# Attention beside a long convolution on one core: narrower convolution matmuls, kv stores in load order, and an earlier table for the short filter

## The chip, the cores and the metric

The kernel runs on one core of one Trainium2 chip. The metric is the device time of one execution in microseconds (us); the time before is the median of three runs, 858.24 us. TensorE is called PE (PEld is its weight load), VectorE DVE, ScalarE ACT, GpSimd POOL, and SyncE, which issues most DMAs, SP. "PEq", "SPq" and so on are the sequencers of these engines.

## The reference

Two independent halves, each over S = 2048 rows and D = 640 channels in bfloat16, are concatenated along the channels:

```python
# A: a short filter, a gate, and a long causal convolution per channel
k_shift = sum_t k[s - t, :] * shift_k[:, t]            # t = 0..3
kv = k_shift * v
y[s, c] = sum_{u <= s} kv[u, c] * ssm_k[c, s - u]      # by FFT in the reference
y = y + kv * ssm_D
a = q * y
# B: softmax attention, 32 heads of 20 channels
q, k, v = (x @ wqkv), split into heads
o = softmax(q k^T * 20**-0.5) v
b = o @ wo
out = concatenate([a, b], axis=-1)
```

## The kernel before

**A planner writes the program.** The class `Prog` keeps a list of instructions for each engine and a modelled clock for each. `build_kernel` walks PE's modelled time forward and, step by step, picks what PE does next; DVE, POOL and SP get their work when the model says that it is ready. The result is a fixed order on each engine, with semaphore waits between them. Constants such as `CQ`, `ZTH`, `ZLO`, `KV0` and `KVS` are the planner's costs, thresholds and due times, so that a changed constant reorders instructions throughout.

**Attention.** Queries are taken in four chunks of 512 (qc), heads in eight groups of four (g), keys in 16 blocks of 128 (kb). A score tile is one head, 128 keys by 512 queries: there are 2048 of them, counted from 0 in the order in which PE makes them. Two or three tiles fill PSUM banks 0 to 2 or 3 to 5 (`S_task`, L619). ACT turns two or three at once into exps in SBUF (`EXP_task`, L661). One tile in seven is given to DVE instead: L681 takes it out of PSUM, and a chain of L716, L717, L718, L719, L721 and L711 or L713, mostly for two tiles at once, makes its exp. `PV_task` (L739) multiplies the exps with V into bank 6; DVE moves that out (L749), and later steps normalise, transpose and multiply with Wo. 36 slots of 512 columns hold exps until PV has read them (32 until the convolution starts).

**Projections.** Q, K (L473) and V (L522) are made from the transposed x as needed, g by g. Their due times are in units of four tiles. DVE copies them from PSUM (L462, L527).

**The first half.** `k_load` brings chunks of 512 rows of k (transposed by the DMA) and of v. `C_task` (L550) applies the short filter on PE: for each of four shifts it multiplies with a diagonal matrix, the table `Dg`, which POOL builds by one instruction from the identity and the filter `SK` (L592). DVE multiplies by v into the tile `kvst` (L570), and SP writes it to `kvr_scratch` in HBM, its rows turned within blocks of 32. There are 20 C tasks, due at `KV0 + KVS * n`. POOL issues the DMAs that copy the long filter into `kext_scratch` (L579 to L590).

**The convolution.** Once all is stored, `conv_setup` clears the tile `KVr` on POOL (L926), loads 80 channels of kv (`kvr_load`), and then 40 tasks of 16 channels run between the other work (`conv_task`, L974): 128 matmuls each, with 128 columns of weights from shifted rows of the long filter (`hk_load`, four DMAs for four channels). POOL arranges the moving columns (`kvx_build`, L948). Each matmul but the first of a task reads twice as many columns as it has data: the second half comes from a tile of zeros, `KVZ`, and adds nothing, but keeps PE's array streaming:

```python
rhs = sub(KVX[i], [[(2 - i) * KVX_E - p, 1 if st else 2], [64, 2], [2, n]], p)
o = sub(bank[MISC], [[-16 if u + x else 16, 1 if st else 2], [256, 2], [1, n]], (4 * u + x) * 16 + d)
```

Here n is 16 - d, with d from 0 to 3. Besides these, `zeros` (L381) multiplies a zero tile with 512 zero columns where PE waits and its planned share of streaming within 3.4 us (`share`) is low. DVE takes the result out (L990, L991, L993); after every tenth task `A_start` loads q, POOL multiplies (L1015) and SP stores the first half.

**What sets the order around the change.** At the start, SP issues the loads of x (`x_load`, transposed), then weights, then SK, k and v. POOL's queue is in the order of `setup_pool`: memsets, the kext DMAs, HD, then Dg. Each DMA on a semaphore waits for the one before it on the same semaphore.

Of the kernel before, what the change touches and what calls it, by code (L numbers as in the profile page):

```python
# [25 lines left out]
NAQ = 6  # L26
# [4 lines left out]
OBS = 20  # L31
NXB = 3
KBV, KBW, LONE = 13, 12, 16
CQ = 0.026
KV0, KVS, VQ, CONVE, ZTH, AGE, WAIT3 = 52, 2.5, 5, 80, 2.1, 40, 0.2
ZST = 6
# [4 lines left out]
PKX, PAT = 0.56, 0.42  # L41
DMAX = 2.0
ZSL, ZLO = 0.45, 1.8
# [43 lines left out]
class Prog:  # L87
# [140 lines left out]
    def dmas(self, eng, pairs, dsem, reads=(), writes=(), slow=1, turn=False):  # L228
# [18 lines left out]
        c = 0.475 * len(pairs)  # L247
# [29 lines left out]
def build_kernel(nc, A_q, A_k, A_v, A_shift_k, A_ssm_k, A_ssm_D, B_x, B_wqkv, B_wo, out):  # L277
# [3 lines left out]
    with ExitStack() as es:  # L281
# [30 lines left out]
        HK_E, KVR_E, KVX_E, Y_E, AST_E = 4 * HKW, 64 * 80, 16 * 64, 16 * 160, 160  # L312
# [14 lines left out]

        WKV = carve(NCC * 2 * D).rearrange("p (c n) -> p c n", c=NCC)
# [3 lines left out]
        kvst = [carve(4 * D).rearrange("p (t d) -> p t d", t=4) for _ in range(2)]  # L332
        pos[0] = 0
        HK = [carve(HK_E) for _ in range(NHK)]
        KVr2 = carve(KVR_E)
# [14 lines left out]
        kvr_d = nc.dram_tensor("kvr_scratch", (S, D), BF16).ap()  # L350
# [49 lines left out]
        for t in range(4):  # L400
            x_load(t, 1)
        x_load(4, 4)
        w_load("sp", [(WKV, D, 2, 0, 160), (WKV, 0, 1, 80, 80), (WQ, 0, 0, 80, 80)], b_Wa, "wa")
# [81 lines left out]
        def prologue():  # L485

            def two(bw, bd):

                bd.w = [t for b in bw for t in b.w]
                bd.r = []  # L490
            for _ in range(ZST):
                zeros(0, 1, True)
            KQ_mm("K", 0, MISC, 0, 384)
            hq, hk = [Buf(), Buf()], [Buf(), Buf()]
            for i, (bk, eng) in enumerate(((4, "dve"), (3, "act"))):
                KQ_mm("Q", 0, bk, 256 * i, 256)
                if i == 0:
                    copy("act", KT[:, 0, 0:384], bank[MISC][:, 0:384], bkb[MISC], hk[0], 0.6)
                copy(eng, QT[:, 0, 256 * i:256 * (i + 1)], bank[bk][:, 0:256], bkb[bk], hq[i], 0.45)
            KQ_mm("K", 0, 5, 384, 128)  # L500
            copy("dve", KT[:, 0, 384:512], bank[5][:, 0:128], bkb[5], hk[1], 0.35)
            two(hq, b_QT[0])
            two(hk, b_KT[(0, 0)])
# [27 lines left out]
        d_kT, d_v, d_kvst = ([DS(n + "0"), DS(n + "1")] for n in ("kT", "v", "kvst"))  # L531
        d_Bs = DS("bs")
        d_kvr, d_sk, d_kext, d_small = DS("kvr"), DS("sk"), DS("kext"), DS("small")
# [6 lines left out]
        def C_task(c, h, bk):  # L540
# [18 lines left out]
            def after():  # L559
                if h < 4:  # L560
                    return
                for t in range(4):
                    bd = Buf()
                    P.dma("sp", ap(kvr_d, [[32 * D, 4], [-D, 32], [1, D]], (c * 512 + t * 128 + 31) * D), kvst[i][:, t, :],
                          d_kvst[i], reads=[b_kvst[i]], writes=[bd])
                    b_kvd.append(bd)
                if c < 2:
                    k_load(c + 2)
# [3 lines left out]
        def setup_pool():  # L572
# [3 lines left out]
            P.dma("sp", SK, ap(A_shift_k, [[KS, 128], [128 * KS, NCC], [1, KS]]), d_sk, writes=[b_SK])  # L576
            k_load(0)
            k_load(1)
# [13 lines left out]
            P.op("pool", lambda e: e.tensor_tensor(  # L592
                Dg, ap(ident, [list(ident.ap[0]), [0, KS], [0, NCC], [1, 128]]),
                ap(SK, [list(SK.ap[0]), [1, KS], [KS, NCC], [0, 128]]), ALU.mult), reads=[b_ident, b_SK], writes=[b_Dg], c=6.0)
# [320 lines left out]
        def conv_setup():  # L915
            allx = [b_WK0, b_WQ0, b_Wa, b_Wb, b_Dg] + b_kT + b_vst + b_kvst
            cv["dead"] = [t for b in allx for t in b.w + b.r]
            cv["HK"] = [Buf(*allx) for _ in range(NHK)]
            cv["KVr"] = Buf(*allx)
# [6 lines left out]
            P.op("pool", lambda e: e.memset(KVr[:, 0:48, :], 0.0), writes=[cv["KVr"]], c=48 * 80 * 0.00095)  # L926
# [6 lines left out]
        def kvr_load(b):  # L933
            P.dmas("sp", [(KVr[32 * a:32 * a + 32, 16 * a:64, :],
                           ap(kvr_d, [[D, 32], [32 * D, 64 - 16 * a], [1, 80]], 80 * b)) for a in range(4)],
                   d_kvr, reads=b_kvd, writes=[cv["KVr"]], slow=2)
# [6 lines left out]
        def kvx_build(t):  # L943
            i = t % 2
            for h in range(2):
                dst = sub(KVX[i].bitcast(U32), [[64, 4], [16, 4], [1, 16]], 256 * h)
                src = sub(KVr2, [[1, 4], [40, 4], [160, 16]], t % 5 * 8 + 4 * h)
                pool_work(lambda e, dst=dst, src=src: e.tensor_copy(dst, src), [cv["KVr"]], [cv["KVX"][i][h]], PKX,  # L948
                          lambda h=h: kvr_load(t // 5 + 1) if h and t % 5 == 4 and t < 39 else None)
# [5 lines left out]
        def conv_task(bt):  # L955
# [3 lines left out]
            for u in range(4):  # L959
# [3 lines left out]
                for x in range(4):  # L963
                    for k in range(8):
# [6 lines left out]
                        rhs = sub(KVX[i], [[(2 - i) * KVX_E - p, 1 if st else 2], [64, 2], [2, n]], p)  # L971
                        o = sub(bank[MISC], [[-16 if u + x else 16, 1 if st else 2], [256, 2], [1, n]], (4 * u + x) * 16 + d)
                        yield (CQ, rd if x + k == 0 else [])
                        P.op("pe", lambda e, o=o, lhsT=lhsT, rhs=rhs, st=st, k=k: e.matmul(  # L974
                            o, lhsT, rhs, start=st, stop=k == 7, skip_group_check=True),
                            reads=rd, writes=[bkb[MISC]], tok=last, c=CQ, st=4 * n / 2400)
# [22 lines left out]
        def A_load(B, tp):  # L999
            i = tp % NAQ  # L1000
            P.dma("sp", Aq[i], ap(q2, [[D, 128], [1, 160]], tp * 128 * D + 160 * B), d_aq[i], writes=[cv["Aq"][i]])

        def A_start(B):

            def go(tp):
                i = tp % NAQ
                q = cv["Aq"][i]
                A_load(B, tp)

                def after():  # L1010
                    P.dma("sp", ap(out2, [[2 * D, 128], [1, 160]], tp * 128 * 2 * D + 160 * B), Aq[i], d_ao[i], reads=[q])
                    if tp + NAQ - 2 < 16:
                        go(tp + NAQ - 2)

                pool_work(lambda e, a=Aq[i], y=Y[B % 2][:, tp, :]: e.tensor_tensor(a, a, y, ALU.mult), [q, cv["Y"][B % 2]], [q], PAT,  # L1015
                          after)

            for tp in range(NAQ - 2):
                go(tp)
# [99 lines left out]
        def dve_run(until):  # L1119
            while True:  # L1120
# [8 lines left out]
                if True:  # L1129
                    fn, rd, wr, c, two = w.steps[w.i]  # L1130
                    t = last_dve[0]
                    last_dve[0] = P.op("dve", fn, reads=rd, writes=wr, c=c, two=two, me=w.steps[w.i])
                    if t and not two:
                        end = st
                        for x in w.steps[w.i:]:
                            if x[4]:
                                break
                            end += x[3] - 0.04
                        if end - st > 0.35:
                            pool_beside(t, st, end)  # L1140
                    w.i += 1
                    if w.i == len(w.steps):
                        works.remove(w)
                        if w.after:
                            w.after()
# [275 lines left out]
```

## Time and profile before

| | |
|---|---|
| median of 3 runs (lowest, highest) | 858.24 us (856.96, 860.21) |
| the profiled execution's own time | 856.55 us |
| its span, first to last instruction | 853.9 us |
| ACT, PE, DVE, POOL busy | 811.3, 819.9, 775.2, 96.4 us |
| exps on ACT (L661): instructions, busy, idle before | 742, 807.8, 26.8 us |
| convolution matmuls (L974) | 5120 |
| zero matmuls (L381) | 230 |
| first exp starts, last exp ends | 10.70, 844.5 us |

A row of a group reads: line, engine, operation, tile written <- tile read, shapes, count, then busy time and mean ns of one, then the engine's idle time just before these instructions and what ended most of it. In the timeline, the first two numbers are start and length, and the bracket holds the idle time before the row's first instruction and its releaser. A busy PE is not a full PE, since matmuls overlap.

### The profile page before, as it was taken

How to read it: one execution, taken by the hardware profiler on the slowest of the kernel's cores; microseconds unless marked ns; L12 is line 12 of the kernel's file. 1: busy time of each engine (PE TensorE's matmuls, PEld its weight loads, DVE VectorE, ACT ScalarE, POOL GpSimd, SP SyncE). 2: the span in 40 equal slices, each digit the busy share in tenths (PEclk: the TensorE clock that was granted, in tenths of full speed). 3: DMA queues.
4: the chain of work that ended last, by engine and by line, in shares of the span. 5: the costliest groups of instructions: out<-in, count | busy, mean ns of one | idle time of the engine just before them, and what ended most of it. 6: DMA issues, size and time to landing. Idle time of an engine off the chain costs nothing.

```text
span 853.9 us, 27281 instructions
## 1 busy us (share of the span) xinstructions
PE 819.9 (96%) x11683; PEld 380.6 (45%) x11694; DVE 775.2 (91%) x1560; ACT 811.3 (95%) x748; POOL 96.4 (11%) x160
## 2 busy tenths in 40 slices
PE   8979999999999999999999999999999999999997
PEld 3433433442255454444535544554544554455422
DVE  1388999999989999998999999999999999999992
ACT  5878799999999999999999999999999999999996
POOL 2020000000111000012211010230110121100011
PEclk9989999999999999999999999999999999999999
DMA  8920110211749967988988796689798888988411
GB/s 171 295 68 2 38 59 16 79 33 32 145 107 201 185 170 169 182 169 183 200 160 173 169 202 146 171 197 199 178 188 157 192 200 192 163 184 182 76 31 46
DMA packets 189463, 121.91 MB, mean 143 GB/s; under 512 B 98048, under 2 KB 188672, under 8 KB 189344
## 3 DMA queue, kind: packets, MB, share of 16 engines
q1 hardware_dynamic: 187152, 117.06, 64.5%
q0 software_dynamic: 736, 2.75, 0.9%
q8 instruction: 92, 1.51, 0.8%
q10 hardware_dynamic: 1456, 0.37, 0.2%
q14 instruction: 27, 0.22, 0.1%
HBM read 106.83 MB, written 10.61 MB: 138 GB/s over the span
## 4 chain that ended last, share of the span: by engine, by line
PE 50%; ACT 33%; DVE 15%; issue 1%; DMA 0%; SPq 0%; DVEq 0%
ACT R L661 33%; PE PS L974 17%; PE PS L619 15%; PE PS L739 8%; PE PS L473 5%; DVE XV L681 3%; DVE XF L721 2%; PE PS L381 2%; PE PS L825 2%; PE PS L522 1%; DVE R L711 1%; DVE ZS L991 1%; DVE ZS L990 1%; DVE R L993 1%; DVE XF L718 1%
## 5 line engine op out<-in xcount | busy, mean ns | idle before, releaser
L661 ACT ACTIVATE R<-PS 128x1024 bf16<-128x1024 f32 (+1 forms) x742 | 807.8, 1230 | 26.8 <-PE PS L619 25.2
L619 PE MATMUL PS<-QT,KT 20*128 20x512 bf16 x2048 | 288.0, 385 | 15.2 <-ACT R L661 7.1
L974 PE MATMUL PS<-R 128*128 128x60 bf16 (+4 forms) x5120 | 212.1, 195 | 0.2 <-DVE R L993 0.2
L681 DVE TENSOR_SCALAR XV<-PS 128x512 uint16<-128x512 f32 x289 | 197.5, 685 | 16.3 <-PE PS L619 13.3
L974 PEld LDWEIGHTS PS<-R 128*128 128x128 bf16 x5120 | 176.0, 98 | 79.0 <-issue 77.7
L739 PE MATMUL PS<-R,V_sb 128*21 128x512 bf16 x2048 | 168.2, 385 | 9.3 <-DVE R L713 5.6
L619 PEld LDWEIGHTS PS<-QT,KT 20*128 20x128 bf16 x2048 | 71.9, 91 | 189.3 <-ACT R L661 131.7
L721 DVE TENSOR_TENSOR XF<-XF 128x1024 bf16<-128x1024 bf16 x145 | 103.6, 716 | 0.3
L718 DVE TENSOR_TENSOR XF<-XF 128x1024 bf16<-128x1024 bf16 x145 | 98.4, 683 | 0.2
L948 POOL COPY R<-R 128x256 uint32<-128x256 uint32 x80 | 51.1, 638 | 377.6 <-DVE XF L721 114.1
L739 PEld LDWEIGHTS PS<-R,V_sb 128*21 128x21 bf16 x2048 | 37.8, 89 | 82.1 <-issue 40.6
L381 PE MATMUL PS<-Zt 128*128 128x512 bf16 x230 | 69.0, 396 | 1.6 <-DVE Zt L375 1.0
L711 DVE TENSOR_TENSOR R<-XF,XV 128x1024 uint16<-128x1024 bf16 x92 | 63.0, 686 | 0.2
L719 DVE TENSOR_SCALAR XF<-XF 128x1024 bf16<-128x1024 uint16 x145 | 60.5, 419 | 0.4
L717 DVE TENSOR_SCALAR XF<-XF 128x1024 bf16<-128x1024 uint16 x145 | 59.9, 420 | 0.1
L716 DVE TENSOR_SCALAR XF<-XV 128x1024 uint16<-128x1024 uint16 x145 | 59.7, 419 | 0.2
L473 PE MATMUL PS<-xT,WQ 128*20 128x512 bf16 (+1 forms) x660 | 51.1, 386 | 1.5 <-DVE XV L681 0.8
L1015 POOL TENSOR_TENSOR R<-R 128x160 bf16<-128x160 bf16 x64 | 31.2, 487 | 160.7 <-DVE XF L719 50.8
L473 PE MATMUL PS<-xT,R 128*20 128x512 bf16 (+2 forms) x660 | 47.3, 378 | 1.1 <-DMA xT<-in_B_x_dram 0.5
L713 DVE TENSOR_TENSOR R<-XF,XV 128x512 uint16<-128x512 bf16 x105 | 40.5, 419 | 0.1
L462 DVE CAST KT<-PS 128x512 bf16<-128x512 f32 (+1 forms) x32 | 21.6, 675 | 14.0 <-PE PS L473 13.6
L749 DVE CAST OT_sb<-PS 128x512 bf16<-128x512 f32 x32 | 21.8, 682 | 12.8 <-PE PS L739 12.8
(54 smaller groups left out, 359.9 us busy)
## 6 DMA issues: line engine op xcount, KB each, us to landing
R<-kext_scratch SPq DMA_DIRECT2D x640, 136.0 KB, 3.7
R<-in_A_v_dram SPq DMA_DIRECT2D x4, 640.0 KB, 6.4
kext_scratch<-in_A_ssm_k_dram POOLq DMA_DIRECT2D x1, 2560.0 KB, 13.2
kvr_scratch<-R SPq DMA_DIRECT2D x16, 160.0 KB
R<-kvr_scratch SPq DMA_DIRECT2D x8, 320.0 KB, 6.2
R<-in_A_q_dram SPq DMA_DIRECT2D x64, 40.0 KB, 3.6
out_dram<-R SPq DMA_DIRECT2D x64, 40.0 KB, 3.2
R<-kvr_scratch SPq DMA_DIRECT2D x8, 240.0 KB, 6.9
```

What stands on the lines that cost most here:

```text
L381: P.op("pe", lambda e: e.matmul(bank[bk], Zt, zrhs, start=start, stop=start, skip_group_check=True), reads=[b_Zt], writes=[bkb[bk]], tok=s ...
L473: ins = e.matmul(bank[bk][32 * i:32 * i + DH, 0:n], Wt[:, cc, off + i * DH:off + (i + 1) * DH], xT[:, cc, x0:x0 + n], start=(cc == 0), sto ...
L619: ins = e.matmul(bank[b0 + i], KT[32 * u:32 * u + DH, g, kb * 128:(kb + 1) * 128], QT[32 * u:32 * u + DH, qs(qc, g), :], start=True, stop= ...
L661: P.op("act", lambda e: e.activation(P_sb[:, s0:s0 + m, :], PS[:, b0 * 512:(b0 + m) * 512].rearrange("p (u q) -> p u q", u=m), ACT.Exp, sc ...
L681: work(0.2, [(lambda e: e.tensor_scalar(V, bank[bk], scale * 1.4426950408889634 * 128.0, 127.0 * 128.0, op0=ALU.mult, op1=ALU.add), [bkb[b ...
L711: last = [(lambda e: e.tensor_tensor(o, Q2, V2, ALU.add), bv + [bq], [b_P[z] for z in zs], two, True)]
L717: (lambda e: e.tensor_scalar(Q, F.bitcast(U16), -128.0, None, op0=ALU.add), [bf], [bq], one, True),
L718: (lambda e: e.tensor_tensor(Q, Q, F.bitcast(U16), ALU.mult), [bf, bq], [bq], two, True),
L719: (lambda e: e.tensor_scalar(F, F.bitcast(U16), a / 16384.0, b / 128.0, op0=ALU.mult, op1=ALU.add), [bf], [bf], one, True),
L721: (lambda e: e.tensor_tensor(Q, Q, F, ALU.mult), [bf, bq], [bq], two, True)] + last, end)
L739: ins = e.matmul(bank[OBANK][32 * u:32 * u + DH + 1, :], V_sb[:, kb, 4 * g + u, :], P_sb[:, slot[4 * b + u], :], start=first, stop=last, t ...
L974: P.op("pe", lambda e, o=o, lhsT=lhsT, rhs=rhs, st=st, k=k: e.matmul(o, lhsT, rhs, start=st, stop=k == 7, skip_group_check=True), reads=rd ...
```

## The change

- **Zero columns.** A convolution matmul reads the second, zero half only for d = 1 and 2, and only where the planned share is under `ZDU`. The planner counts `CQ` for a narrow and `CQD` for a wide one. Thresholds of the zero matmuls move (`ZTH`, `ZSL`, `ZLO`).
- **Prologue.** x's first 512 rows come by two loads of 256, K and Q of the first group in two halves each, with 7 and 4 zero matmuls ahead of them.
- **SK and Dg.** SK's load is issued after x's first eight tiles of 128 rows. Dg's multiply stands ahead of the kext DMAs on POOL. `k_load(1)` moves behind the small loads.
- **kv stage.** `kvst` lies under `KVr` rather than beside the other old tiles, with a semaphore for each row tile (eight in all). C tasks are due at 48 + 2 n rather than 52 + 2.5 n.
- **kv in HBM.** `kvr_scratch` has the order of its loads: for each of eight channel groups, 32 rows of 64 x 80 values. Each of the 16 row tiles is stored by eight DMAs of 80 channels; a load reads one run for each partition.
- **The clearing of KVr** goes in four pieces to the queue of POOL work that the planner puts beside DVE. The q loads and stores of the first half take two row tiles each.
- **Other planner constants**, in the diff's first part.

```diff
-NAQ = 6
+NAQ = 3
-OBS = 20
+OBS = 28
-KBV, KBW, LONE = 13, 12, 16
-CQ = 0.026
-KV0, KVS, VQ, CONVE, ZTH, AGE, WAIT3 = 52, 2.5, 5, 80, 2.1, 40, 0.2
-ZST = 6
+KBV, KBW, LONE = 12, 12, 24
+CQ, CQD, ZDU = 0.0258, 0.0304, 2.1
+KV0, KVS, VQ, CONVE, ZTH, AGE, WAIT3 = 48, 2.0, 5.5, 100, 2.2, 40, 0.2
+ZST = 7, 4
-PKX, PAT = 0.56, 0.42
-DMAX = 2.0
-ZSL, ZLO = 0.45, 1.8
+PKX, PAT = 0.64, 0.49
+DMAX = 2.5
+ZSL, ZLO = 0.3, 1.4
...
-        c = 0.475 * len(pairs)
+        c = (0.475 if len(pairs) < 8 else 0.545) * len(pairs) if not turn else 0.4 + 0.0068 * pairs[0][1].shape[0]
...
+        kvst = [carve(4 * D).rearrange("p (t d) -> p t d", t=4) for _ in range(2)]
         WKV = carve(NCC * 2 * D).rearrange("p (c n) -> p c n", c=NCC)
...
-        kvst = [carve(4 * D).rearrange("p (t d) -> p t d", t=4) for _ in range(2)]
         pos[0] = 0
+        KVr2 = carve(KVR_E)
         HK = [carve(HK_E) for _ in range(NHK)]
-        KVr2 = carve(KVR_E)
...
-        kvr_d = nc.dram_tensor("kvr_scratch", (S, D), BF16).ap()
+        kvr_d = nc.dram_tensor("kvr_scratch", (8, 32, 64, 80), BF16).ap()
...
-        for t in range(4):
-            x_load(t, 1)
+        x_load(0, 2)
+        x_load(2, 2)
         x_load(4, 4)
+        d_sk = DS("sk")
+        P.dma("sp", SK, ap(A_shift_k, [[KS, 128], [128 * KS, NCC], [1, KS]]), d_sk, writes=[b_SK])
...
-            for _ in range(ZST):
-                zeros(0, 1, True)
-            KQ_mm("K", 0, MISC, 0, 384)
...
+            for i, (bq, bk) in enumerate(((4, MISC), (3, 5))):
+                for _ in range(ZST[i]):
+                    zeros(i, 1, True)
+                KQ_mm("Q", 0, bq, 256 * i, 256)
+                copy("dve", QT[:, 0, 256 * i:256 * (i + 1)], bank[bq][:, 0:256], bkb[bq], hq[i], 0.45)
+                KQ_mm("K", 0, bk, 256 * i, 256)
+                copy("act", KT[:, 0, 256 * i:256 * (i + 1)], bank[bk][:, 0:256], bkb[bk], hk[i], 0.45)
...
+        d_kvst = [DS("kvst%d" % n) for n in range(8)]
...
-                    P.dma("sp", ap(kvr_d, [[32 * D, 4], [-D, 32], [1, D]], (c * 512 + t * 128 + 31) * D), kvst[i][:, t, :],
-                          d_kvst[i], reads=[b_kvst[i]], writes=[bd])
+                    P.dmas("sp", [(ap(kvr_d, [[80, 4], [-5120, 32], [1, 80]], ((32 * n + 31) * 64 + 16 * c + 4 * t) * 80),
+                                   kvst[i][:, t, 80 * n:80 * n + 80]) for n in range(8)], d_kvst[4 * i + t], reads=[b_kvst[i]], writes=[bd])
...
+            P.op("pool", lambda e: e.tensor_tensor(
+                Dg, ap(ident, [list(ident.ap[0]), [0, KS], [0, NCC], [1, 128]]),
+                ap(SK, [list(SK.ap[0]), [1, KS], [KS, NCC], [0, 128]]), ALU.mult), reads=[b_ident, b_SK], writes=[b_Dg], c=4.7)
             k_load(0)
-            k_load(1)
...
-            P.op("pool", lambda e: e.tensor_tensor(
-                Dg, ap(ident, [list(ident.ap[0]), [0, KS], [0, NCC], [1, 128]]),
-                ap(SK, [list(SK.ap[0]), [1, KS], [KS, NCC], [0, 128]]), ALU.mult), reads=[b_ident, b_SK], writes=[b_Dg], c=6.0)
+            k_load(1)
...
-            P.op("pool", lambda e: e.memset(KVr[:, 0:48, :], 0.0), writes=[cv["KVr"]], c=48 * 80 * 0.00095)
+            for i in range(4):
+                pool_work(lambda e, i=i: e.memset(KVr2[:, 480 * i:480 * i + 480], 0), [], [cv["KVr"]], 0.55)
...
-            P.dmas("sp", [(KVr[32 * a:32 * a + 32, 16 * a:64, :],
-                           ap(kvr_d, [[D, 32], [32 * D, 64 - 16 * a], [1, 80]], 80 * b)) for a in range(4)],
-                   d_kvr, reads=b_kvd, writes=[cv["KVr"]], slow=2)
+            P.dmas("sp", [(KVr[32 * a:32 * a + 32, 16 * a:64, :].rearrange("p j c -> p (j c)"),
+                           ap(kvr_d, [[5120, 32], [1, (64 - 16 * a) * 80]], 163840 * b)) for a in range(4)],
+                   d_kvr, reads=b_kvd, writes=[cv["KVr"]])
...
-                        rhs = sub(KVX[i], [[(2 - i) * KVX_E - p, 1 if st else 2], [64, 2], [2, n]], p)
-                        o = sub(bank[MISC], [[-16 if u + x else 16, 1 if st else 2], [256, 2], [1, n]], (4 * u + x) * 16 + d)
+                        m = 2 if d in (1, 2) and share(P.T["pe"]) < ZDU else 1
+                        rhs = sub(KVX[i], [[(2 - i) * KVX_E - p, m], [64, 2], [2, n]], p)
+                        o = sub(bank[MISC], [[-16 if u + x else 16, m], [256, 2], [1, n]], (4 * u + x) * 16 + d)
...
-                            reads=rd, writes=[bkb[MISC]], tok=last, c=CQ, st=4 * n / 2400)
+                            reads=rd, writes=[bkb[MISC]], tok=last, c=CQ if m == 1 else CQD, st=2 * m * n / 2400)
```

## The prediction

> **What bounds the kernel now.** I read the page's busy shares first, then the costliest groups by form, then the timeline wherever ACT stood still.
>
> ```profile
> PE 819.9 (96%) x11683; PEld 380.6 (45%) x11694; DVE 775.2 (91%) x1560; ACT 811.3 (95%) x748; POOL 96.4 (11%) x160
> ...
> L661 ACT ACTIVATE R<-PS 128x1024 bf16<-128x1024 f32 (+1 forms) x742 | 807.8, 1230 | 26.8 <-PE PS L619 25.2
> ```
>
> Three engines are nearly full. The exps on ACT (L661) set the pace: the first starts at 10.70 us, the last ends at 844.5, and 9.4 us of tail follow. In the timeline, exps back to back start 0.908 us apart (two tiles) or 1.331 us (three tiles), so 465 and 276 of them need 422 + 367 = 790 us. They take 833.8, so 44 us are lost, of which the page shows 26.8 as idle; the rest are delays shorter than ACT's pipeline. Summing what each start-to-start distance has over those two numbers puts 20 us before 100 us, 2.6 between 100 and 210, and 22 between 210 and 800. Only these can be won without moving work off ACT. All wait for scores (L619): PE was late.
>
> The longest loss is one event:
>
> ```profile
> 53.60 5.35 DVE L721 TENSOR_TENSOR XF<-XF 128x1024 bf16<-128x1024 bf16 x1
> 53.78 4.62 POOL L592 TENSOR_TENSOR R<-ident,SK 128x2560 bf16<-128x2560 bf16 x1
> ...
> 59.58 1.46 PE L739 MATMUL PS<-R,V_sb 128*21 128x512 bf16 x12 [4.33 <-DVE R L713]
> ...
> 61.63 1.02 ACT L661 ACTIVATE R<-PS 128x1024 bf16<-128x1024 f32 x1 [5.00 <-PE PS L619]
> ```
>
> L721 takes 0.68 us elsewhere. Here it runs beside POOL's multiply that builds Dg (L592) and takes 5.35. PE's PV waits for it, scores queue behind PV, ACT starves. Four-us windows show PE's clock drop too:
>
> ```profile
> 52.00:56.00 4.00, 3.03 (x29) 1.30 (x26) 4.00 (x7) 4.00 (x6) 3.16 (x3) 1.00 0.06 2
> 56.00:60.00 4.00, 0.42 (x8) 0.15 (x12) 4.00 (x5) 0.63 (x1) 2.39 (x1) 0.63 0.00 0
> 60.00:64.00 4.00, 4.00 (x37) 0.61 (x29) 2.75 (x6) 1.89 (x2) 0.00 (x0) 0.51 0.02 4
> ```
>
> After the counts in brackets come clock, DMA share and GB/s. The second large loss lies at 79 to 92 us:
>
> ```profile
> 84.32 3.28 ACT L661 ACTIVATE R<-PS 128x1536 bf16<-128x1536 f32 x3 [3.07 <-PE PS L619]
> ...
> 91.97 9.64 ACT L661 ACTIVATE R<-PS 128x1024 bf16<-128x1024 f32 x9 [4.37 <-PE PS L619]
> ```
>
> There PE runs K, Q and C matmuls in one piece between two scores.
>
> **What the Trainium skill says.** "SBUF — State Buffer", section "Who interferes with whom": a DVE instruction with two SBUF inputs contends with a GpSimd instruction that reads SBUF, not with one that only writes it; one with at most one SBUF input, outside two-port modes, does not contend. The trace agrees: L721 stretched to 5.35; L462 and L681 (PSUM input) take 0.68 with POOL busy beside them; L711 takes 0.69 beside the memset L926. "TensorE: Matmul & The Clock Gate", "What's actually happening": the clock falls to half after an idle window of about 3.4 us. Here 0.63 and 0.51 over two 4 us windows mean some 7 us at half rate. Same page, "Wait — 56ns, not 53.3ns?": starts of matmuls come no closer than about 25 ns.
>
> **The change, part by part.** Counts are from the order of the built instructions.
>
> 1. Dg moves ahead of the kext DMAs on POOL and needs only SK, whose load moves up on SP behind x's first eight tiles. SK is issued near 9 us and has landed near 17 (7.7 us to landing before), so Dg runs near 17 to 22. DVE then has only L462/L527 casts from PSUM; chains start near 40. Gain: the excess of exp starts from 54 to 64 us, 6.0. Ends: 4 (some delay remains) to 6. Passed on the queues: SK's issue (0.94 us on SP) delays the wqkv loads and x tiles 8 to 15; K's matmuls on x tiles 8 to 11 start at 19.4 and the last x tile landed by 20.5 for use at 23.3, so 1 us is hidden. POOL's kext DMAs start some 2 us later and are needed after 200 us. k_load(1) after Wo and HD: first used near tile 190, hidden. **-6.0.**
>
> 2. ACT: 274 exps of three tiles for 276, 466 of two for 465; DVE takes 293 tiles for 289. 2 x 1.331 - 0.908 = **-1.8.** DVE in turn: +4 x 0.685 for L681; 141 full and 11 single chains for 144 and 1; 47 instructions more in all, +14 us by the rows' means, less some 4 of overlap between neighbours: +10. DVE idles 600 - 578.4 = 21.6 us between 200 and 800, so most hides; delays of 0 to 4, I take **+1.**
>
> 3. Convolution, narrow matmuls: 3110 have 26 to 32 columns, 2010 still twice as many; before, all but 40 were wide. What a narrow one saves no row tells well:
>
> ```profile
> L974 PE MATMUL PS<-R 128*128 128x52 bf16 x1280 | 151.6, 197 | 0.0
> ...
> L974 PE MATMUL PS<-R 128*128 128x64 bf16 x1240 | 150.0, 195 | 0.0
> ...
> 349.53 1.07 PEld L974 LDWEIGHTS PS<-R 128*128 128x128 bf16 x33 [0.23 <-issue]
> ```
>
> 33 weight loads in 1.07 us are 30 ns each, and over all runs I get 31.5. Width 52 is no quicker than 64, so the weight load may set the pace (saving 0); the page's 25 ns gives 6.5 x 3070 = 20 us of PE time. I take 3 ns: 9. A third of PE relief should reach ACT, as its 22 us lost there come from PE lateness mixed with DVE's. **-3**, ends 0 and -8. The 34 more zero matmuls (264 for 230, 7.3 us) fill waits; if not, they take the gain back.
>
> 4. C tasks earlier (tiles 145 to 357, before 141 to 405). Long PE blocks between scores, before: 3.95 and 4.84 us (tiles 141, 149); now 3.48 (tile 304: 11 V matmuls x 0.137, 16 L550 x 0.056, 20 of K at 0.217 per four) and 6.64 (tile 320). ACT lost the block less 0.5 to 0.9; so 7.4 go and some 8.7 come. **+1.2**, ends -1 and +3.
>
> 5. kv stores: 16 of 128 rows become 128 of 160-byte runs. Before, each waited for the last on its semaphore:
>
> ```profile
> SPq L234 <- DMA kvr_scratch<-R: 40.6, 12, 4.3
> ```
>
> Now eight leave together, 32 per chunk at 0.43 to 0.54 us: 17 us of SP, like 4 x 4.3 before. Queued behind: v of the next chunk but one. 17.3 + 2.7 (transposed k) + 6.4 (landing) = 26 us against 58 tiles x 0.407 (834/2048) = 24 plus part 4's 9: hidden by about 6 us; if not, DVE, being in order, waits in L570. The last 64 stores (35 us) leave about 20 us before the convolution at tile 505, so they may cost 0.85 each. Store price of short runs is not in the trace: **0**, ends 0 and +6.
>
> 6. At nothing: contiguous kv loads and A in pairs (L974 idles 0.2 us, never for POOL or DMA); KVr's memset in four. The prologue: 13 + 4 zero matmuls, Q and K halves reach the first score at about 10.2 us, as before (10.27), with x's second pair landed near 7.5. The half-clock window at 12 to 16 (0.59) may go: **-0.5**, ends 0 and -1.5.
>
> Sum: -6.0 - 1.8 + 1 - 3 + 1.2 - 0.5 = -9.1: span 844.8, own time 856.55 - 9.1 = 847.5. The profiled run lay 1.7 under the median, so **849**.
>
> **The rivals.** *The relief carries through*: narrow matmuls at 25 ns and half of 20 us reaching ACT, with DVE hiding its share: 7 + 1 more, 841. For it: 22 us lost to late scores. Against: 52 columns no quicker than 64.
> *The gain is spent again*: narrow saves nothing, zero matmuls, DVE's chains and the 6.64 block cost 4 to 9: 853 to 858. The change then doesn't do what its first words say.
> *The clock falls in the convolution*, the case on the other side. The change drops 88,900 columns, at 0.42 ns (0.215 us for 512) 37 us of 600, and returns 7.3. If PE then looks idle in a window, it runs at half rate for 3.4 us and does up to 1.7 us less. Place: the 600 us of L974. Against: clock 1.00 in every window from 64 to 850, though the trace does not tell the margin. At six such windows of 170 the 9 us are gone, at nine the kernel is slower; a dozen give 860.
>
> **How the numbers follow.** Forecast 0.60, relief 0.14, spent 0.16, clock 0.10. Half a per cent, 4.3 us, is about what a measurement of this kernel tells from no change. The forecast's part bounds give 842 to 854; adding most of "spent" above, 842 to 858. Faster: the forecast nearly whole, relief, a little of spent: 0.76. Same 0.14, slower 0.10.
>
> **What would show it.** Right: Dg before 25 us, L721's mean near 0.68, no ACT gap between 50 and 65, ACT gaps of 3 and 6 near tiles 304 to 320, weight loads of L974 closer than 30 ns, clock 1.00 throughout. Wrong: a clock under 1 after 64 us, PE waiting for KVX at the convolution's start, DVE's L570 waiting for v, or ACT losing over 22 us between 210 and 800.

## Result, and the profile after

The changed kernel takes **837.84 us** (median of four runs, 837.40 to 838.12). The kernel before took 858.40 beside it (four runs, 856.96 to 860.21). The ratio is 0.9759 with the interval [0.974, 0.9778]: 20.6 us less, where the prediction had 9 and a range from 842 to 858. The profiled execution took 837.92 us, its span is 836.1.

I read the page's busy shares and the exps' row first (busy time, share of the span and instructions; then busy us, mean ns | idle us before them):

```profile
PE 811.6 (97%) x11716; PEld 367.5 (44%) x11728; DVE 776.1 (93%) x1608; ACT 802.1 (96%) x747; POOL 95.1 (11%) x163
...
L660 ACT ACTIVATE R<-PS 128x1024 bf16<-128x1024 f32 (+1 forms) x741 | 798.8, 1300 | 18.4 <-PE PS L618 17.9
```

The exps (L660, before L661) ran 9 us less, and the idle time before them fell by 8. But the mean of one *rose*, from 1230 to 1300 ns, with hardly another mix of two and three tiles. In the trace exps overlap: back to back they start 0.905 us apart, while one of two tiles lasts 1.14 us on the mean (1.08 before). So an exp whose scores are ready is counted from a time when the one before it still runs, and a longer mean with less idle time says that scores came early more often. The chain that ended last (the work followed back from the last instruction, as shares of the span) says the same, of before and then of after:

```profile
PE 50%; ACT 33%; DVE 15%; issue 1%; DMA 0%; SPq 0%; DVEq 0%
```

```profile
ACT 45%; DVE 31%; PE 22%; issue 1%; DVEq 0%
```

The sum that the prediction used, of what each exp's distance to the next start has over the back-to-back distance (here 0.905 us for two tiles, where the prediction had 0.908, and 1.331 for three), tells where the time came from. I call it ACT's loss:

| us of the span | before | after |
|---|---|---|
| 0 to 40 | 5.8 | 5.8 |
| 40 to 64 | 6.0 | 0.3 |
| 64 to 100 | 8.2 | 0.4 |
| 100 to 210 | 2.6 | 13.3 |
| 210 to 800 | 21.9 | 9.4 |
| after 800 | 0.3 | 0.3 |
| sum | 44.9 | 29.4 |

The span fell by 17.8: 15.4 from the loss, 1.75 from two exps of three tiles fewer and one of two tiles more, and 0.7 from the first exp's start (10.47 for 10.70) and the tail (8.9 for 9.4). Up to 20.6, 0.8 lies outside the span (the profiled executions' own times differ by 18.6), and the profiled execution of before lay 1.9 us under that median.

**The stall at 54 us is gone.** In ACT's timeline (start, length, then the row; the bracket would hold idle time before it):

```profile
49.86 51.13 ACT L660 ACTIVATE R<-PS 128x1024 bf16<-128x1024 f32 x50
```

Fifty exps follow one another from 49.86 to 101. Dg's multiply (L576, L592 before) now stands at

```profile
10.56 4.48 POOL L576 TENSOR_TENSOR R<-ident,SK 128x2560 bf16<-128x2560 bf16 x1 [6.07 <-DMA SK<-in_A_shift_k_dram]
```

**The blocks of projections and C tasks moved.** Of the 13.3 us lost between 100 and 210 us, 10.7 are three gaps, in brackets:

```profile
133.04 7.38 ACT L660 ACTIVATE R<-PS 128x1536 bf16<-128x1536 f32 x7 [1.14 <-PE PS L618]
143.56 6.88 ACT L660 ACTIVATE R<-PS 128x1024 bf16<-128x1024 f32 x6 [3.13 <-PE PS L618]
156.89 3.77 ACT L660 ACTIVATE R<-PS 128x1024 bf16<-128x1024 f32 x4 [6.44 <-PE PS L618]
```

Ahead of the last one PE ran this (timeline of the changed kernel):

```profile
150.88 1.26 PE L475 MATMUL PS<-xT,WQ 128*20 128x512 bf16 x20
...
152.07 0.85 PE L521 MATMUL PS<-R,xT 128*128 128x320 bf16 x5
...
152.76 0.83 PE L550 MATMUL PS<-R 128*128 128x128 bf16 x12
...
154.39 1.26 PE L475 MATMUL PS<-xT,R 128*20 128x512 bf16 x20
...
155.58 0.62 PE L550 MATMUL PS<-R 128*128 128x128 bf16 x8
...
156.45 0.60 PE L618 MATMUL PS<-QT,KT 20*128 20x512 bf16 x6 [0.25 <-DVE KT L464]
```

Q, V, a C task, K and the next C task stand between two scores (L618), which themselves need the K just made.

**The largest part lies in the convolution.** The groups on ACT between 210 and 800 us, of before and then of after:

```profile
L661 ACT ACTIVATE R<-PS 128x1024 bf16<-128x1024 f32 (+1 forms) x531 | 584.8, 1226 | 6.5 <-PE PS L619 5.0
```

```profile
L660 ACT ACTIVATE R<-PS 128x1024 bf16<-128x1024 f32 (+1 forms) x543 | 590.8, 1314 | 1.2 <-PE PS L618 0.7
```

In the same 590 us ACT now does 12 exps more. This is the part that the prediction put at 2 us. The groups on PE in that stretch show the widths of the convolution's matmuls:

```profile
L976 PE MATMUL PS<-R 128*128 128x26 bf16 x1280 | 136.5, 178 | 0.0
L976 PE MATMUL PS<-R 128*128 128x32 bf16 x1280 | 136.1, 178 | 0.0
...
L976 PE MATMUL PS<-R 128*128 128x56 bf16 x1001 | 120.3, 194 | 0.0
L976 PE MATMUL PS<-R 128*128 128x60 bf16 x1009 | 120.0, 193 | 0.0
L381 PE MATMUL PS<-Zt 128*128 128x512 bf16 x196 | 56.1, 383 | 0.9 <-DVE R L995 0.9
```

The mean of one (178 for 194) is not the price of one, since they overlap. From start to start inside runs of them, a narrow one takes 25.0 ns (median; mean 26 to 28), a wide one of 56 or 60 columns 30; over all runs 28.2 ns, where it was 31.55. Times 5120 that is 144.4 us of PE for 161.5.

PE's clock was at half only from 12.34 to 15.75 us and after 834.95. In two kernels among the experiments some executions had it at half for tens of us; they are named there.

### The profile page after: what moved, and what is told of

Same layout as the page of the kernel before. It is cut to its first block, busy times and chain, and to the rows that moved or that the text cites. A ratio compares the mean times of both kernels' runs of the same rounds, so it can differ in the third digit from the quotient of the medians.

```text
span 836.1 us, 27480 instructions
## 1 busy us (share of the span) xinstructions
PE 811.6 (97%) x11716; PEld 367.5 (44%) x11728; DVE 776.1 (93%) x1608; ACT 802.1 (96%) x747; POOL 95.1 (11%) x163
## 3 DMA queue, kind: packets, MB, share of 16 engines
q8 instruction: 93, 1.52, 0.8%
## 4 chain that ended last, share of the span: by engine, by line
ACT 45%; DVE 31%; PE 22%; issue 1%; DVEq 0%
ACT R L660 45%; DVE XV L680 7%; PE PS L618 7%; PE PS L976 5%; DVE XF L717 3%; DVE XF L720 3%; PE PS L738 3%; PE PS L475 3%; DVE XF L715 2%; DVE R L710 2%; DVE XF L718 2%; DVE XF L716 2%; PE PS L381 2%; DVE R L712 2%; PE PS L521 1%; DVE ZS L993 1%
## 5 line engine op out<-in xcount | busy, mean ns | idle before, releaser
L660 ACT ACTIVATE R<-PS 128x1024 bf16<-128x1024 f32 (+1 forms) x741 | 798.8, 1300 | 18.4 <-PE PS L618 17.9
L618 PE MATMUL PS<-QT,KT 20*128 20x512 bf16 x2048 | 287.2, 385 | 14.0 <-ACT R L660 6.2
L976 PEld LDWEIGHTS PS<-R 128*128 128x128 bf16 x5120 | 161.9, 97 | 89.3 <-issue 88.6
L976 PE MATMUL PS<-R 128*128 128x32 bf16 (+5 forms) x5120 | 197.4, 184 | 0.0
L618 PEld LDWEIGHTS PS<-QT,KT 20*128 20x128 bf16 x2048 | 71.7, 91 | 187.8 <-ACT R L660 144.0
L720 DVE TENSOR_TENSOR XF<-XF 128x1024 bf16<-128x1024 bf16 (+1 forms) x152 | 101.1, 665 | 0.3
L717 DVE TENSOR_TENSOR XF<-XF 128x1024 bf16<-128x1024 bf16 (+1 forms) x152 | 100.8, 664 | 0.2
L381 PE MATMUL PS<-Zt 128*128 128x512 bf16 x264 | 77.4, 393 | 1.9 <-DVE Zt L375 1.0
L718 DVE TENSOR_SCALAR XF<-XF 128x1024 bf16<-128x1024 uint16 (+1 forms) x152 | 62.2, 409 | 0.2
L716 DVE TENSOR_SCALAR XF<-XF 128x1024 bf16<-128x1024 uint16 (+1 forms) x152 | 61.2, 408 | 0.1
L715 DVE TENSOR_SCALAR XF<-XV 128x1024 uint16<-128x1024 uint16 (+1 forms) x152 | 60.9, 407 | 0.2
L1015 POOL TENSOR_TENSOR R<-R 128x160 bf16<-128x160 bf16 x64 | 31.2, 488 | 165.3 <-DVE XF L717 43.8
L475 PE MATMUL PS<-xT,R 128*20 128x512 bf16 (+1 forms) x660 | 47.2, 379 | 0.0
L712 DVE TENSOR_TENSOR R<-XF,XV 128x512 uint16<-128x512 bf16 x119 | 45.7, 417 | 0.2
L381 PEld LDWEIGHTS PS<-Zt 128*128 128x128 bf16 x264 | 17.9, 99 | 36.2 <-issue 26.3
```

Source lines behind the costliest of these rows:

```text
L381: P.op("pe", lambda e: e.matmul(bank[bk], Zt, zrhs, start=start, stop=start, skip_group_check=True), reads=[b_Zt], writes=[bkb[bk]], tok=s ...
L475: ins = e.matmul(bank[bk][32 * i:32 * i + DH, 0:n], Wt[:, cc, off + i * DH:off + (i + 1) * DH], xT[:, cc, x0:x0 + n], start=(cc == 0), sto ...
L618: ins = e.matmul(bank[b0 + i], KT[32 * u:32 * u + DH, g, kb * 128:(kb + 1) * 128], QT[32 * u:32 * u + DH, qs(qc, g), :], start=True, stop= ...
L660: P.op("act", lambda e: e.activation(P_sb[:, s0:s0 + m, :], PS[:, b0 * 512:(b0 + m) * 512].rearrange("p (u q) -> p u q", u=m), ACT.Exp, sc ...
L715: (lambda e: e.tensor_scalar(F.bitcast(U16), V, 127, None, op0=ALU.bitwise_and), bv, [bf], one, True),
L716: (lambda e: e.tensor_scalar(Q, F.bitcast(U16), -128.0, None, op0=ALU.add), [bf], [bq], one, True),
```

## Experiments

**My theory after the result** was that the scores between 210 and 800 us come earlier because the convolution's matmuls take less of PE. **The rival** was that they come earlier because the plan is true: before, the planner counted 26 ns (`CQ`) for a matmul that takes 31.55, so that over 5120 of them its PE clock runs 28 us ahead of the chip's; the change's 25.8 and 30.4 ns fit. Other parts (Dg, kv's order, due times, DVE's constants) were tried apart. "Order pinned" means that every engine has its instructions in the order of the kernel named.

### e1: Dg early, alone

The kernel before, with the order of all else pinned through the planner's times.

```diff
+            P.op("pool", lambda e: e.tensor_tensor(
+                Dg, ap(ident, [list(ident.ap[0]), [0, KS], [0, NCC], [1, 128]]),
+                ap(SK, [list(SK.ap[0]), [1, KS], [KS, NCC], [0, 128]]), ALU.mult), reads=[b_ident, b_SK], writes=[b_Dg], c=6.0)
...
-            P.op("pool", lambda e: e.tensor_tensor(
-                Dg, ap(ident, [list(ident.ap[0]), [0, KS], [0, NCC], [1, 128]]),
-                ap(SK, [list(SK.ap[0]), [1, KS], [KS, NCC], [0, 128]]), ALU.mult), reads=[b_ident, b_SK], writes=[b_Dg], c=6.0)
...
```

> The kernel before with one edit: POOL's multiply that builds Dg stands ahead of the kext DMAs, and every other instruction of all five engines keeps its place. Theory 'the stall is a loss of its own': L721 falls back to 0.68 us, the ACT gap of 5.0 us at 57 us and the half clock there go, and the kernel takes 6 us less (852 to 853). Rival 'the stall only hides another wait': the next wait on PE or DVE takes its place and less than 2 us is gained.

Measured: 850.15 us against 857.41, 0.9911 [0.9887, 0.9936]: 7.3 less, of which 5.7 show as loss in the profiled execution. The loss from 40 to 64 us is 0.3 for 6.0; from 210 to 800 it stays at 22.5. In the timeline of e1 (its L726 is L721 of before) the instruction that took 5.35 us is back at its length, and ACT runs through:

```profile
53.48 0.68 DVE L726 TENSOR_TENSOR XF<-XF 128x1024 bf16<-128x1024 bf16 x1
```

```profile
38.99 27.97 ACT L666 ACTIVATE R<-PS 128x1536 bf16<-128x1536 f32 x27
```

The stall is a loss of its own, and taking it away gives the convolution nothing.

### e2: the changed kernel with wide matmuls

Order pinned to the changed kernel; narrow and wide are counted as there, but all are emitted wide.

```diff
-                        rhs = sub(KVX[i], [[(2 - i) * KVX_E - p, m], [64, 2], [2, n]], p)
+                        w = 1 if st else 2
+                        rhs = sub(KVX[i], [[(2 - i) * KVX_E - p, w], [64, 2], [2, n]], p)
...
```

> The changed kernel with its order of instructions kept, but every convolution matmul (all but the first of a task) reads the zero half again. Theory 'narrow matmuls carry the gain of the convolution stage': PE gets back 3070 times 5 to 6.5 ns, 15 to 20 us, and the time rises by 7 to 12 us. Rival 'the new order carries it': the time rises by less than 3 us.

Measured: 842.12, 0.982 [0.9785, 0.9855], 4.3 over the changed kernel. A matmul takes 31.5 ns again, and PE 17 us more, but the loss from 210 to 800 rises only by 5.8, to 15.2: a third of it. (The median time rises by less: three of its four executions have a clock of 1.000, where all four of the changed kernel have 0.997 or 0.998. The one with 0.998 took 843.52, or 5.7 more.) Narrowness on this order is worth some 6 of 12.5 us. Neither theory alone gives that.

### e3: the kernel before with narrow matmuls

Order pinned to the kernel before; only d = 1 and 2 stay wide.

```diff
+                        w = 2 if d in (1, 2) else 1
-                        rhs = sub(KVX[i], [[(2 - i) * KVX_E - p, 1 if st else 2], [64, 2], [2, n]], p)
+                        rhs = sub(KVX[i], [[(2 - i) * KVX_E - p, w], [64, 2], [2, n]], p)
...
```

> The kernel before with its order kept, but convolution matmuls with d = 0 and 3 read no zero half (2560 narrow, 2560 wide). Theory 'narrow matmuls carry the gain': 2520 times 5 to 6.5 ns less on PE, and 5 to 10 us less in all. Rival 'the new order carries it': less than 2 us. Rival 'the clock': fewer columns than in any run so far and no zero matmuls in return, so the clock falls under 1 in some windows and the kernel gets slower by 3 us or more.

Measured: 846.67, 0.9868 [0.9833, 0.9904], 10.7 less. A matmul takes 28.9 ns, so PE saves 13.6 us, and the loss from 210 to 800 is 13.0, or 8.9 less. Here two thirds of PE's relief reach ACT, on the order that counts 26 ns for each.

### e4: the kernel before with another price

One constant; all matmuls stay wide.

```diff
-CQ = 0.026
+CQ = 0.0315
```

> The kernel before with one constant changed: the planner counts 31.5 ns for a convolution matmul, as the trace of before shows it, rather than 26. Widths stay. Theory 'the plan of before was wrong about PE, and a plan with true costs is the gain': 6 to 10 us less. Rival 'widths carry it': within 2 us of before, since PE has the same work.

Measured: 844.14, 0.9844 [0.9806, 0.9882]: **13.3 less, and no matmul is shorter** (31.57 ns from start to start). The loss from 210 to 800 is 10.9. ACT's group in that stretch, then the zero matmuls of the whole run:

```profile
L661 ACT ACTIVATE R<-PS 128x1024 bf16<-128x1024 f32 (+1 forms) x544 | 588.6, 1313 | 2.7 <-PE PS L619 2.1
```

```profile
L381 PE MATMUL PS<-Zt 128*128 128x512 bf16 x146 | 44.8, 403 | 1.0 <-DVE Zt L375 1.0
```

544 exps with a mean of 1313 ns, as in the changed kernel; 146 zero matmuls, where it was 230. A true price is enough to halve this loss.

### e5: the changed kernel with prices too low

Both prices are 18% lower, the width rule stays.

```diff
-CQ, CQD, ZDU = 0.0258, 0.0304, 2.1
+CQ, CQD, ZDU = 0.0213, 0.0249, 2.1
```

> The changed kernel with the planner's two prices of a convolution matmul set as far below the trace as the old one was: 21.3 and 24.9 ns for 26.6 and 30.2. Widths follow the same rule (1435 wide for 2010). Theory 'a plan that undercounts PE is what cost the convolution stage': zero matmuls go from 264 to 377, scores come late again, and 8 to 14 us are lost (846 to 852). Rival 'the old constants were only a bad draw of the planner': within 3 us of the changed kernel.

Measured: 849.35, 0.9912 [0.9897, 0.9927], 11.5 over the changed kernel, though more of its matmuls are narrow (3685 for 3110) and one takes 27.4 ns. The loss from 210 to 800 is 20.4. The same two views as for e4:

```profile
L660 ACT ACTIVATE R<-PS 128x1024 bf16<-128x1024 f32 (+1 forms) x531 | 585.9, 1236 | 6.1 <-PE PS L618 3.9
```

```profile
L381 PE MATMUL PS<-Zt 128*128 128x512 bf16 x377 | 109.7, 389 | 1.4 <-DVE Zt L375 1.0
```

ACT is back at 531 exps, and the planner spends the time that it thinks PE has on zero matmuls, 109.7 us of them. This is nearly the time of e1, which has Dg early and the old price.

### e6 and e8: other due times for the C tasks

```diff
-KV0, KVS, VQ, CONVE, ZTH, AGE, WAIT3 = 48, 2.0, 5.5, 100, 2.2, 40, 0.2
+KV0, KVS, VQ, CONVE, ZTH, AGE, WAIT3 = 52, 2.5, 5.5, 100, 2.2, 40, 0.2
```

> The changed kernel with the C tasks due as before (52 + 2.5 n). The longest PE blocks between scores before the convolution are 2.18 and 4.18 us in place of 3.48 and 6.64. Theory 'ACT loses a block less half a us': about 4 us less lost at tiles 280 to 330, so 833 to 835. Rival 'the later start of the convolution (tile 527 for 505) costs as much': 838.

Measured: 835.78, 0.9757 [0.974, 0.9775], 2.1 under the changed kernel. The loss from 64 to 210 is 12.9 for 13.7, with gaps of 4.30 and 1.28 where 6.44 and 3.13 were; it is shared out otherwise rather than gone. Most of the 2.1 lies elsewhere, at the start: in e6's profiled execution PE's clock is not at half at 12 us, the first exp starts 0.5 earlier, and the loss up to 40 us is 4.5 for 5.8. Two of e6's executions have a clock of 1.000 and took 834.8 and 835.0; the other two have 0.997 and 0.998, as all four of the changed kernel do, and took 836.5 and 836.9. So the due times are worth about 1 us, where 4 was expected.

e8 goes on in that direction:

```diff
-KV0, KVS, VQ, CONVE, ZTH, AGE, WAIT3 = 48, 2.0, 5.5, 100, 2.2, 40, 0.2
+KV0, KVS, VQ, CONVE, ZTH, AGE, WAIT3 = 56, 3.0, 5.5, 100, 2.2, 40, 0.2
```

> The changed kernel with C tasks due at 56 + 3 n: one block of 4.17 us is left before the convolution, which starts at tile 569 and ends at tile 1990. Theory 'blocks cost ACT their length': 7 us less lost before 200 us, 830 to 832. Rival 'the convolution is then squeezed': its end at tile 1990 brings the first half's last stores into the tail, or PE is too full after tile 569, and the time is 836 or more.

Measured: 837.59 (four runs, 834.93 to 849.93), 0.9764 [0.9744, 0.9785]. The loss from 100 to 210 falls to 7.1 from 13.3, but the time doesn't fall to the 830 to 832 of the expectation: the best execution took 834.93, level with e6's best, and what takes the place of the 6 us there has no trace. The run of 849.93 is the profiled one: PE's clock is at half from 364.47 to 405.43 us. Outside that spell its loss is that of the changed kernel (2.7 for 2.7 us between 210 and 361, 6.8 for 6.2 between 410 and 800), so it gives the rival, a squeezed convolution, no support. Stretches of that trace (length, busy us of PE, PEld, DVE, ACT and POOL with counts, then the clock, DMA share and GB/s):

```profile
300.00:360.00 60.00, 58.17 (x968) 28.98 (x968) 59.40 (x126) 59.86 (x55) 5.72 (x9) 1.00 0.83 181
360.00:410.00 50.00, 48.48 (x557) 19.42 (x554) 34.79 (x69) 36.75 (x32) 4.50 (x8) 0.59 0.60 130
410.00:460.00 50.00, 48.38 (x781) 23.80 (x779) 49.61 (x103) 49.80 (x47) 10.89 (x20) 1.00 0.87 187
```

PE counts as busy through the spell, yet does 557 matmuls in the 50 us where it does 781 in the next 50; ACT starves. Against the run of 834.93 (clock 1.00 on average) it is 15 us for twelve windows of 3.41 us (the length of the half-rate stretch at 12.34 in the changed kernel), 1.25 us each. Just ahead of the spell PE stands still for 1.52 us between two matmuls of the convolution, waiting for nothing that the profile shows, and is busy for only 1.89 of 3.41 us:

```profile
363.39 0.25 PE L976 MATMUL PS<-R 128*128 128x26 bf16 x4 [1.52 <-issue]
```

```profile
361.06:364.47 3.41, 1.89 (x45) 1.32 (x45) 1.89 (x5) 2.20 (x3) 0.00 (x0) 1.00 1.14 216
```

### e7: kv in HBM in rows

The changed kernel with kv as before: 16 stores of whole rows, loads in runs of 160 bytes. Planned durations are kept, so PE, DVE, ACT and POOL keep their orders.

```diff
-        kvr_d = nc.dram_tensor("kvr_scratch", (8, 32, 64, 80), BF16).ap()
+        kvr_d = nc.dram_tensor("kvr_scratch", (S, D), BF16).ap()
...
-                    P.dmas("sp", [(ap(kvr_d, [[80, 4], [-5120, 32], [1, 80]], ((32 * n + 31) * 64 + 16 * c + 4 * t) * 80),
-                                   kvst[i][:, t, 80 * n:80 * n + 80]) for n in range(8)], d_kvst[4 * i + t], reads=[b_kvst[i]], writes=[bd])
+                    P.dmas("sp", [(ap(kvr_d, [[32 * D, 4], [-D, 32], [1, D]], (c * 512 + t * 128 + 31) * D), kvst[i][:, t, :])],
+                           d_kvst[4 * i + t], reads=[b_kvst[i]], writes=[bd],
...
```

> The changed kernel with kv in HBM in rows of 640 channels as before: 16 stores of 1280-byte runs and loads of 160-byte runs, each row tile's store on a semaphore of its own; the order on all other engines is kept. Theory 'the order of kv in HBM is hidden': within 1 us of 837.8. Rival 'loads of short runs make the moving columns late': L976 or L948 waits for the load after every fifth task, up to 7 times 1 to 2 us.

Measured: 838.09, 0.978 [0.9766, 0.9795]; the changed kernel's time within 0.3 us, and the losses are the same stage by stage. The order of kv in HBM costs nothing and brings nothing.

### e9: three edits of the change, the rest as before

Dg early, the width rule and its prices (25.8 and 30.4 ns) in the kernel before; thresholds, prologue, kv and due times as before.

```diff
-CQ = 0.026
+CQ, CQD, ZDU = 0.0258, 0.0304, 2.1
...
+                        m = 2 if d in (1, 2) and share(P.T["pe"]) < ZDU else 1
...
```

> The kernel before with three edits alone: Dg ahead of the kext DMAs, the rule for narrow convolution matmuls, and their prices 25.8 and 30.4 ns in the planner. Prologue, C tasks' due times, kv's order in HBM, KVr's memset and all other constants stay as before. Theory 'these three are the whole gain': 7 us from Dg and 12 to 13 between 210 and 800 us, so 837 to 839, level with the changed kernel. Rival 'the rest of the change adds to it': 842 or more.

Measured: 849.32 (six runs, 838.0 to 853.42), 0.9841 [0.9793, 0.9888]. The runs differ by their clock: 838.0 with a mean of 0.999, 840.5 with 0.994, and 849 to 853 with 0.970 to 0.978. The profiled one has two spells at half rate in the convolution:

```profile
660.00:684.00 24.00, 23.67 (x248) 8.77 (x244) 16.49 (x36) 17.68 (x15) 3.83 (x8) 0.50 0.71 160
...
790.00:803.00 13.00, 13.00 (x168) 6.21 (x166) 9.53 (x21) 9.80 (x9) 0.00 (x0) 0.50 0.18 32
```

In the one execution with a nearly full clock (838.0) the three edits give the whole gain. The profiled one agrees: outside its spells it loses 8.3 us between 210 and 655 and 1.1 between 690 and 786, the changed kernel 7.7 and 1.3. But here the clock often falls. Which of the change's other edits keeps it up wasn't tried.

**What stands ahead of the falls.** I take windows of 3.41 us on the grid of each trace's own falls and estimate how long PE streamed in each: 0.42 ns for a column (0.215 us for 512), overlapping matmuls counted once. In the window ahead of e8's spell that gives 1.0 us, ahead of e9's two 1.7 and 1.5, and ahead of the stall's half rate in before 0.8. These are the least of their traces. Between 20 and 820 us of all 14 traces, no window above 1.7 us was followed by a fall, and just two below it (1.64 each) were not followed by one. The changed kernel's least window has 1.8. So a fall follows a window in which PE streams for less than about half the time, even where it counts as busy for 2.73 of 3.41 us, as ahead of e9's first spell. Why the half rate then lasts from 7 to 41 us is open.

### e10, e11: prices fitted and too high

Both with the due times of e6; the prices of e10, then of e11:

```diff
-CQ, CQD, ZDU = 0.0258, 0.0304, 2.1
+CQ, CQD, ZDU = 0.0272, 0.0308, 2.1
```

```diff
-CQ, CQD, ZDU = 0.0258, 0.0304, 2.1
+CQ, CQD, ZDU = 0.0295, 0.0335, 2.1
```

> The changed kernel with C tasks due at 52 + 2.5 n and the prices of a convolution matmul at 27.2 and 30.8 ns, nearer to the 28.2 ns that its runs take on the mean. Theory 'each step towards the true price helps': 1 to 2 us less than the due times alone gave (835.8), so 834 to 835. Rival 'the remaining error is within the noise of the plan': 835 to 838.

> As the one before it, but prices some 10% too high: 29.5 and 33.5 ns. Theory 'only undercounting hurts': a plan that takes PE for slower than it is puts in fewer zero matmuls (188) and moves no score late, so within 1.5 us of the true prices. Rival 'any error hurts, up or down': 3 us or more slower, as PE then waits for exps that the plan put later.

Measured: e10 839.80 (836.67 to 840.04), 0.978 [0.9759, 0.9801]; e11 836.68, 0.9752 [0.9735, 0.9769]. Against e6's 835.78, on another chip, neither gains; for e10 both theory and rival had less. Its profiled execution (837.88) has the loss of e6 and lies 2.9 over e6's: the first exp starts 1.2 later, the tail is 0.5 longer, and four more exps, with fewer of three tiles, take some 1.1. Its three executions near 840 have a clock of 0.996, the two below 838 of 0.999 and 1.000. e11 counts 10% too much and loses nothing by it: in these runs only a price that is too low hurts.

### e12: DVE's constants as before

```diff
-OBS = 28
+OBS = 20
-KBV, KBW, LONE = 12, 12, 24
+KBV, KBW, LONE = 13, 12, 16
-KV0, KVS, VQ, CONVE, ZTH, AGE, WAIT3 = 48, 2.0, 5.5, 100, 2.2, 40, 0.2
+KV0, KVS, VQ, CONVE, ZTH, AGE, WAIT3 = 48, 2.0, 5, 80, 2.2, 40, 0.2
-PKX, PAT = 0.64, 0.49
+PKX, PAT = 0.56, 0.42
```

> The changed kernel with the planner's constants for DVE's and POOL's work as before (KBV 13, LONE 16, VQ 5, CONVE 80, OBS 20, PKX 0.56, PAT 0.42). Blocks before the convolution are 4.79, 3.78 and 5.69 us for 3.48 and 6.64. Theory 'prices carry the convolution stage': as good there as the changed kernel (loss from 210 to 800 us under 11), and 3 us more in the blocks, so 840 to 842. Rival 'these constants carry it': the loss from 210 to 800 us rises to 15 or more, 845 or over.

Measured: 841.82, 0.9817 [0.9796, 0.9838], 4 over the changed kernel. The loss from 100 to 210 us is 17.1 for 13.3, with gaps of 4.52, 3.60 and 5.05 where the plan has blocks of 4.79, 3.78 and 5.69; from 210 to 800 it is 10.1 for 9.4. These constants help around the blocks, not in the convolution.

### What they say together

"Uncounted" is 5120 times the measured distance from start to start, less what the planner counted for the same matmuls:

| kernel | ns measured | ns counted (mean) | uncounted, us | ACT's loss, 210 to 800 |
|---|---|---|---|---|
| before | 31.55 | 26.0 | 28.4 | 21.9 |
| e1 | 31.55 | 26.0 | 28.4 | 22.5 |
| e5, low prices | 27.4 | 22.3 | 26.2 | 20.4 |
| e2, after, wide | 31.5 | 27.6 | 20.2 | 15.2 |
| e3, before, narrow | 28.9 | 26.0 | 14.8 | 13.0 |
| after | 28.2 | 27.6 | 3.1 | 9.4 |
| e6, due times | 28.3 | 27.6 | 3.3 | 9.3 |
| e4, before, price | 31.57 | 31.5 | 0.3 | 10.9 |
| e11, high prices | 28.5 | 31.2 | -13.8 | 8.4 |

The loss follows the fourth column, not the second: e4 and before have the same matmuls and lose 10.9 and 21.9; after and e5 have nearly the same and lose 9.4 and 20.4. e7, e10 and e12, whose uncounted time is within some 3 us of nothing, lose 9.6, 9.3 and 10.1. The number of zero matmuls doesn't order them: after has 264 and before 230. Narrow matmuls gain most where they bring the chip to what the plan counts (e3). So the two cures don't add: in this stage e3 gives 8.9, e4 11.0, and the change, which has both, 12.5. From 8.4 to 10.9 us stay wherever the price is not too low, and why isn't shown.

One rival to the change's first words is open: e1 (7.3) and e4 (13.3) sum to the 20.6 us of the whole change, with all matmuls wide. They weren't run together, so whether narrow matmuls are needed at all isn't shown.

How a low price delays the scores is argued, not shown step by step: the orders are fixed, so what the planner puts on PE in time that isn't there stands ahead of the next scores. e5's zero matmuls are the visible part; e3 keeps all 230 of them and still gains, so they are not all of it.

## Why the prediction was wrong, step by step

The sign was right, the size was not. The forecast's path held at each sign that it named: Dg before 25 us, the chain's instruction at its usual length (its row's mean is 665 ns), no gap between 50 and 65, gaps of 3 and 6 us, weight loads closer than 30 ns (median 26), a full clock after 16 us. None of its signs of error appeared. One step failed.

- **Step 1, Dg (-6.0): right.** 5.7 in the changed kernel's table, 7.3 for e1 alone. SK landed sooner than I put it, Dg ran at 10.56 and not at 17 to 22. The Trainium skill, "SBUF — State Buffer", section "Who interferes with whom", has the contention of two readers of SBUF that the prediction leaned on; before and e1 agree: 5.35 us beside POOL's multiply, 0.68 without.
- **Step 2, exps (-1.8, DVE +1): right for ACT**, -1.75. DVE was to be busy for 10 us more; it is for 0.9, or 5.6 without the instruction that was stretched. What that costs ACT can't be told apart from step 3.
- **Step 3, convolution (-3): the step that failed.** With DVE's +1 the sum had -2 for 210 to 800 us; the trace has -12.5. A narrow matmul was put at 3 ns less, 9 us of PE in all; the trace has 17.1 us less. Narrow ones start every 25.0 ns (median; mean 26 to 28) where a matmul took 31.5. The median is at the floor of about 25 ns of "TensorE: Matmul & The Clock Gate", section "Wait — 56ns, not 53.3ns?", which I had named as the other end; that 52 columns are no quicker than 64 (33 and 34 ns) didn't mean that 26 are not. And "a third of PE relief should reach ACT" had no row behind it: on the new order a third does (e2), on the order of before two thirds (e3). The largest term was missing, put at nothing: **I had 31.5 ns from the trace and `CQ = 0.026` in the diff, and did not set them side by side.** That is 5.5 x 5120 = 28 us of PE that the plan didn't know of, and it caused about half of the 22 us of late scores: with the price alone put right, 10.9 remain (e4). The price alone gives what the forecast gave to the whole change, and more.
- **Step 4, blocks (+1.2): within its ends.** 7.8 went between 64 and 100 us and 10.7 came between 100 and 210: +2.9. The gaps of 3.13 and 6.44 are the blocks that the prediction named (3.48 and 6.64 us).
- **Step 5, kv stores (0): right**, as e7 shows. No PE wait for KVX appeared.
- **Step 6, prologue (-0.5): missed by little.** The first exp is 0.23 earlier; the half-rate window at 12 to 16 stayed.

**The rivals.** *The relief carries through* (841, chance 0.14) was nearest, and still short: it had more of the same PE time, and not the price. *The gain is spent* did not happen. *The clock falls* did not happen to the changed kernel, but does to near neighbours: e8 in one run of four, e9 in most. Its price, up to 1.7 us per window, is 1.25 by e8, and a dozen windows gave 850 for 835, so the rival deserved its tenth. (Its own sum was off: a dozen at up to 1.7 is 20 us, up to 869 and not 860.) The same TensorE page, section "What's actually happening", ties half rate to an idle window of about 3.4 us. These traces agree in part: the windows ahead of the spells were not idle, with PE busy for 1.89 (e8), 2.73 and 2.52 of 3.41 us (e9), but they are those in which it streamed least. The margin that the prediction said the trace does not tell can thus be estimated: 1.8 us in the changed kernel's least window, where 1.5 to 1.7 fell in e9.

The range failed for the same reason: no part stood for the plan coming true. Nor does its lower end follow from the parts: with each at its own low end they sum to -18.3, which gives 840 and not 842, and the measured time is below that too.

## What to carry to other kernels

Where a planner or a model orders the work, compare each of its prices with the start-to-start distance in the trace before pricing anything else, and multiply the difference by the count: here one constant was worth as much as narrower matmuls. A price that is too low puts work in front of what the critical engine waits for; one that is 10% too high cost nothing in the one run that tried it (e11). And when a stage's loss has no single event behind it, bound the whole of that loss as a possible gain.

## What the runs showed of the hardware

- A weight load of 128 columns with a matmul of 28 to 32 columns starts every 25.0 ns (median, changed kernel); with 56 or 60 columns every 29 to 31, with 52 or 64 every 33 to 34 (before). With 26 columns the median is 25 in the changed kernel and 30 in e3. The widths are not in order, so the column count alone doesn't set it.
- PE's clock can stay at half for 24 (e9) and 41 us (e8) while PE counts as busy and work is waiting, and then return under the same kind of work; the kernel lost 1.25 us per 3.41 us window (e8). Each fall between 20 and 820 us followed a window in which PE streamed for an estimated 0.1 to 1.7 of 3.41 us; ahead of e8's it stood still for 1.52. The same program has executions without such a spell.
- 128 stores of 160-byte runs from SP, hidden beside other work, cost the kernel nothing measurable against 16 stores of whole rows (838.09 and 837.84).
